# Order of the last pair of an MLP's first product, and one of two left sums moved to VectorE

## The chip, the cores and the metric

The kernel runs on one core of a Trainium2 chip. Five engines work side by side, each through its own queue in order: TensorE (PE in the profile; PEld is its loading of weights), VectorE (DVE), ScalarE (ACT), GpSimd (POOL) and SyncE (SP), whose queue here only issues DMAs. ACT issues DMAs too, for what it has just computed. The metric is the time of the whole program on the device in microseconds (us), lower being better.

## The reference

A transformer block on 2048 tokens of width 1024, in float32: attention with a memory carried over four segments, and then an MLP with 3584 inner features. The change lies in the MLP:

```python
def _B_ref(x, w1, b1, w2, b2):
    y = _layernorm(x, axis=-1)
    h = _gelu(jnp.einsum("bsd,df->bsf", y, w1) + b1)
    return jnp.einsum("bsf,fd->bsd", h, w2) + b2

h2 = h + _B_ref(_layernorm(h, axis=-1), B_w1, B_b1, B_w2, B_b2)
```

`h @ w2` is the MLP's second product, `y @ w1` its first.

## The kernel before

Every matrix product runs in three passes, since each operand x is split into a high part (`hi`, a cast to the format of the matmul, on ACT) and a low part (`x - hi`, a subtraction on DVE): high by high, high by low, low by high. Both products of the MLP use a scheme with seven block products in place of eight (Strassen's, in Winograd's form), so sums and differences of blocks are formed first.

*First product.* The tokens come in two halves. In each half, `Mixer.pair(j)` makes a pair of 128-row blocks of h, for j from 0 to 13, out of block products of 12 matmuls each. It is a generator that yields after every three matmuls, and the main loop hangs other work at these points, written (j, n): pair j, n-th yield. In the last pair of the second half (j = 13, `HP - 1`) there are 16 points: 0 to 3 multiply into the bank `bps`, then DVE reads `bps` (L1037); 4 to 7 multiply into the bank `dps`, then DVE reads it (L906), ACT applies the GELU (L899) and issues the store of h; 8 to 11 go on in `bps`, which DVE then reads; 12 to 15 go on in `dps`, which DVE then reads. A matmul that goes on in a bank waits for the read before it.

*Second product.* Class `Second` holds it. There are 112 products (`jobs`) of 21 matmuls, 56 for each of two halves of the inner features. In a half they go by groups of block products: "1" with "7", "6" with "5", "3" with "2", and "4". In a group the products of eight pairs of token blocks alternate. I number the products 0 to 111; the group of "6" and "5" is products 16 to 31 and 72 to 87. Its helpers are:

- `load_rows` and `rows_ahead` load rows of W2 into four buffers, on SP's queue. `presum` forms a sum of two rows on POOL where the block wants one (L1135). `fill` makes a piece of W2 of a row: the cast on ACT (L1143), the subtraction on DVE (L1144), and for some a store for later use on SP's queue (L1146). `fill_up(n, most)` makes all pieces due by product n, at most `most` of them.
- `load_items` loads the left blocks of h, named `hr`, into six buffers on SP's queue (L1171). `sums` forms their sums (L1189 for "1", L1192 and then L1193 for "6", L1198 for "3"), all on POOL. For "6" the result of L1192 is the left operand of "5" and the result of L1193 that of "6"; the latter is also stored (to `s2_dram`, shown as `s_dram`, at L1256) for the group of "3", and its buffer is loaded again once that store has landed.
- `prep(n)` makes the left operand of product n: a cast on ACT (L1212) and a subtraction on DVE (L1213).
- `add` adds a finished bank to one or two blocks of the output, on DVE (L1282). These blocks, `c`, are loaded by `ahead`.

`run` names, for each product n, first its matmuls and then `work(n)`: rows and loads on SP, sums due by product n + 2, `prep(n + 2)`, the additions of product n, the pieces of W2 due by now, and sums due by n + 4. Everything from the last part of the layer norm on is under `in_order()`, which binds each engine to the order in which the code names its instructions. So a line that is named earlier stands earlier in its engine's queue, and on SP's queue a DMA that waits for a buffer holds all that are named behind it.

Product 2, ("7", 0), goes on in the bank of product 0, so its first matmul waits for the additions of product 0. Of the 14 pieces of W2 that products 0 to 3 need, four remain for the last pair; two of them have rows in buffers of another pool (`APART`, shown as w2s).

Of the kernel before, what the change touches and what calls it, by code (L numbers as in the profile page):

```python
# [13 lines left out]
ALU = mybir.AluOpType  # L14
# [29 lines left out]
def build(tc, x, wq, wk, wv, wo, beta, w1, b1, w2, b2, out):  # L44
    nc = tc.nc
# [147 lines left out]
    def chain(*gens):  # L193
        for g in gens:
            yield from g
# [136 lines left out]
    def attention_pool(half):  # L332
        ab = acts["ab"] = tc.alloc_tile_pool(name=f"ab{half}", bufs=1, reuse_waits="tile")
        mask = acts["mask"] = ab.tile([P, 512], F32, name="mask")
        nc.gpsimd.memset(mask, 0.0)
        nc.gpsimd.affine_select(mask[:, 384:512], mask[:, 384:512], pattern=[[-1, P]],
                                compare_op=ALU.is_ge, fill=-1e9 / SCALE, base=0, channel_multiplier=1)
        acts["mz"] = ab.tile([P, NG * 132 + 96], F32, name="MZ")
        if half == 0:
            nc.gpsimd.memset(acts["mz"], 0.0)  # L340
        else:
            nc.sync.dma_start(acts["mz"], mz_dram)
# [350 lines left out]
    def load_x(half, sl, hts):  # L693
        for t in range(4):
            r0 = half * HT + (4 * sl + t) * P
            nc.sync.dma_start(hts[t], x[0, r0:r0 + P, :])
# [176 lines left out]
    HP = FB // 2  # L873
# [175 lines left out]
    class Second:  # L1049
# [129 lines left out]
        def sums(self, n, due):  # L1179
            tt = nc.gpsimd.tensor_tensor  # L1180
            while self.ns < self.ni and self.items[self.ns][0] <= due:
                at, s, g, p = self.items[self.ns]
                if at > n + 2 and self.came[s, g, p] >= n:
                    break
                r = {w: self.raws.pop((s, g, p, w)) for w in self.LOADS[g]}
                t = {w: x[0] for w, x in r.items()}
                self.ns += 1
                if g == "1":
                    tt(t["21"], t["11"], t["21"], op=ALU.subtract)  # L1189
                    src = ("1", "11"), ("7", "21")  # L1190
                elif g == "6":
                    tt(t["21"], t["21"], t["22"], op=ALU.add)  # L1192
                    tt(t["11"], t["21"], t["11"], op=ALU.subtract)  # L1193
                    self.later.append((s2_dram[p], t["11"]))
                    src = ("6", "11"), ("5", "21")
                    self.free.append(r["22"][1])
                elif g == "3":
                    tt(t["s2"], t["12"], t["s2"], op=ALU.subtract)  # L1198
                    src = ("3", "s2"), ("2", "12")
                else:  # L1200
                    src = ("4", "22"),
                for name, w in src:
                    self.srcs[s, name, p] = r[w]
# [95 lines left out]
    for half in range(2):  # L1299
        acts["zt"] = zt = tc.alloc_tile_pool(name=f"zt{half}", bufs=1, side="right")  # L1300
        attention_pool(half)
        first = None if half else opening()
        rest = attention(half, first)
        hts = [lnp.tile([P, D], F32, tag="ln", name="ht0", bufs=4) for _ in range(4)]
        ab = acts["ab"]
        load_x(half, 0, hts)

        def pre():
            for _ in range(PD):
                yield  # L1310
            for g in range(NG - 1):
                load_o(half, 1, g, ab)
                for _ in range(PS):
                    yield

        interleave(wo_first(half, hts, pre()), rest, RA, RH, RS)
        if half == 0:
            nc.sync.dma_start(mz_dram, acts["mz"])
        ab.release()
        zx = acts["zx"] = tc.alloc_tile_pool(name=f"zx{half}", bufs=1, side="right", reuse_waits="tile")  # L1320
        mq = tc.alloc_tile_pool(name=f"mq{half}", bufs=1, side="right", reuse_waits="tile")
        pp = tc.alloc_tile_pool(name=f"post{half}", bufs=1, reuse_waits="tile")
        hts1 = [pp.tile([P, D], F32, name=f"ht1{i}") for i in range(4)]
        acts["b2"] = pp.tile([P, D], F32, name="b2c")
        mixer = Mixer(half, mq)
        last_token = []

        def ready(t):
            steps = ln2_token(half, hts1, pp, t)
            if t < 3:  # L1330
                for _ in steps:
                    pass
            else:
                last_token.append(steps)

        second = wo_second(half, hts1, ready)
        load_x(half, 1, hts1)
        nc.sync.dma_start(acts["b2"], bass.AP(tensor=b2.tensor, offset=b2.offset, ap=[[0, P], [1, D]]))
        with in_order(mybir.EngineType.PE):
            interleave(hooked(second, lambda k: mixer.begin(), 57, 1),  # L1340
                       ln2(half, 0, hts, pp), 0.5)
        acts.pop("last")

        def ln2_last():
            yield
            next(last_token[0])
            side = ln2_combined(half, hts1)
            for n, _ in enumerate(side):
                if n == 1:
                    next(last_token[0])  # L1350
                yield

        order = ExitStack()
        order.enter_context(in_order())
        side, acc = ln2_last(), 0.0
        todo = {11: lambda: mixer.combine(0), 12: lambda: (mixer.fetch(1), mixer.made(0, "S2", "S1", "S3")),
                13: lambda: (mixer.made(0, "A22", "S4"), mixer.combine(1))}
        for _ in mixer.lead():
            acc += 0.4
            while side and acc >= 1.0:  # L1360
                acc -= 1.0
                if next(side, 0) == 0:
                    side = None
                    pp.release()
                    mp = mixer.mp = tc.alloc_tile_pool(name=f"m1{half}", bufs=1, side="right", reuse_waits="tile")
                    mixer.fetch(0)
            if mixer.step in todo and not side:
                todo.pop(mixer.step)()
        assert not todo

        if half == 0:
            for j in range(HP - 9):
                for _ in mixer.pair(j):
                    pass
            acts["ahead"] = ln1(1, 1)
            interleave(chain(*(mixer.pair(j) for j in range(HP - 9, HP))),
                       chain(ln1(1, 0, 2), islice(acts["ahead"], 3)), 0.17)
            mp.release()
            mq.release()
            zx.release()  # L1380
            zt.release()
        else:
            second = Second(mq)
            fill_at = [(j, 5) for j in range(HP - 8, HP - 2)] + [(HP - 3, 13), (HP - 2, 12), (HP - 2, 15), (HP - 2, 18),
                       (HP - 1, 1), (HP - 1, 9), (HP - 1, 13)]
            for j in range(HP):
                if j == HP - 1:
                    mp.release()
                    acts["sp"] = sp = tc.alloc_tile_pool(name="sp", bufs=1, side="right", reuse_waits="tile")
                for n, _ in enumerate(mixer.pair(j)):  # L1390
                    if (j, n) == (HP - 9, 8):
                        second.rows_ahead(-10)
                    if (j, n) == (HP - 1, 0):
                        second.load_items(-2)
                    if (j, n) in ((HP - 1, 6), (HP - 1, 10)):
                        second.sums(0, n // 10)
                    if (j, n) in ((HP - 1, 8), (HP - 1, 12)):
                        second.prep(n // 12)
                    if (j, n) in fill_at:
                        second.fill_up(-8, 1)  # L1400
                        second.rows_ahead(-10)
                    if (j, n) == (HP - 1, 1):
                        second.presum(second.nl)
                    if (j, n) == (HP - 1, 12):
                        second.ahead(-1)
            second.fill_up(-8, 1)
            second.rows_ahead(-10)
            second.prep(2)
            wp.release()
            acts["cl"] = cl = tc.alloc_tile_pool(name="cl", bufs=1, reuse_waits="tile")  # L1410
            cl.tile([P, 512], F32, tag="r", name="c", bufs=4)
            cl.tile([P, 512], F32, tag="w", name="c", bufs=12)
            acts["cx"] = cx = tc.alloc_tile_pool(name="cx", bufs=1, reuse_waits="tile")
            second.run()
        order.close()
# [24 lines left out]
```

## Time and profile before

| | |
|---|---|
| median of 3 runs | 2308.16 us (2304.3 to 2308.86) |
| the profiled execution | 2308.02 us |
| its span, first to last instruction | 2305.8 us |
| granted clock of TensorE | 1.000 |
| PE busy | 2273.6 us, 99% |
| DVE busy | 1546.7 us, 67% |
| ACT busy | 1224.5 us, 53% |
| POOL busy | 1067.9 us, 46% |

The first product of the second half of the tokens ends at about 1762 us, the second product runs from there to the end. In the profile, times are counted from the first instruction. A busy time says how long an engine worked, not whether anyone waited for it; what a stage is limited by is read from the waits of PE in it, which the next section shows.

### The profile page before, as it was taken

The page shows a single profiled execution, that of the slowest core. Times are in us where ns is not written, and L with a number is a line of the kernel's source. Part 1 is how long each engine was busy: PE and PEld are TensorE (multiplying, and loading weights), DVE is VectorE, ACT ScalarE, POOL GpSimd, SP SyncE. Part 2 cuts the span into 40 slices and gives each one's busy share as a digit, 9 for nine tenths or more (in the row PEclk, how much of TensorE's full clock was granted, in tenths as well). Part 3 has the DMA queues.
Part 4 walks back from the last instruction along what each step waited for, and adds up shares of the span by engine and source line. Part 5 has one row for each costly group of instructions (what it writes and reads, how often), then busy time and mean ns, then how long its engine had stood idle before and what let it go on. Part 6 is the DMA issues. An engine that isn't in the chain of part 4 may idle for free.

```text
span 2305.8 us, 35327 instructions
## 1 busy us (share of the span) xinstructions
PE 2273.6 (99%) x11769; PEld 1890.2 (82%) x11769; DVE 1546.7 (67%) x3271; ACT 1224.5 (53%) x2549; POOL 1067.9 (46%) x1084
## 2 busy tenths in 40 slices
PE   8999999999999999999999999999999999999999
PEld 6888888878888888888888877888887878888887
DVE  6777777776655565777777777665566756566553
ACT  5777777775453445777777775363333223322221
POOL 5444555554244442555555546253444554155340
PEclk9999999999999999999999999999999999999999
DMA  6333333335466654433333344466658976476762
GB/s 177 102 84 92 92 85 84 90 110 184 139 208 174 183 169 141 113 92 86 85 89 87 85 113 147 154 210 174 178 174 276 327 243 217 155 244 219 257 235 91
DMA packets 322719, 355.36 MB, mean 154 GB/s; under 512 B 26190, under 2 KB 218730, under 8 KB 322538
## 3 DMA queue, kind: packets, MB, share of 16 engines
q1 hardware_dynamic: 259370, 316.40, 45.2%
q10 hardware_dynamic: 63168, 36.71, 5.3%
q8 instruction: 93, 1.52, 0.3%
q14 instruction: 88, 0.72, 0.1%
HBM read 226.59 MB, written 76.09 MB: 131 GB/s over the span
## 4 chain that ended last, share of the span: by engine, by line
PE 84%; ACT 4%; DMA 3%; DVE 3%; POOL 3%; issue 2%; SPq 1%; ACTq 0%; DVEq 0%; POOLq 0%
PE po L1272 20%; PE bps L882 9%; PE cps L882 7%; PE dps L882 6%; PE ppt L573 5%; PE po L593 5%; PE pqk L541 3%; PE vps L115 2%; PE vps L116 2%; PE vps L117 2%; PE kps L115 2%; PE kps L116 2%; PE kps L117 2%; PE qps L116 2%; PE qps L115 2%
## 5 line engine op out<-in xcount | busy, mean ns | idle before, releaser
L557 POOL TENSOR_SCALAR pr<-pr,nm,gate 128x128 f32<-128x128 f32 (+3 forms) x512 | 321.0, 636 | 355.1 <-DVE nm L554 272.4
L550 ACT ACTIVATE pr<-pr,mx 128x256 f32<-128x256 f32 (+3 forms) x512 | 287.5, 562 | 166.2 <-DVE mx L542 163.2
L580 DVE TENSOR_TENSOR ptl<-ppt,pth 128x512 fp32r<-128x512 f32 (+1 forms) x384 | 227.2, 599 | 73.9 <-ACT pth L575 68.7
L542 DVE CUSTOM_DVE_ANT_0 pr<-pqk,mask 128x256 f32<-128x256 f32 (+3 forms) x512 | 242.8, 484 | 42.7 <-PE pqk L541 40.1
L573 PE MATMUL ppt<-ident,pr 128*128 128x128 f32 x1280 | 223.6, 277 | 2.3 <-POOL pr L557 1.5
L575 ACT CAST pth<-ppt 128x512 fp32r<-128x512 f32 (+1 forms) x384 | 194.2, 517 | 35.5 <-PE ppt L573 29.4
L1282 DVE TENSOR_TENSOR c<-c,po 128x512 f32<-128x512 f32 x160 | 105.3, 682 | 143.8 <-PE po L1272 141.1
L573 PEld LDWEIGHTS ppt<-ident,pr 128*128 128x128 f32 x1280 | 164.1, 140 | 33.5 <-DVE ptl L580 2.8
L541 PE MATMUL pqk<-ks,qs 96*128 96x256 f32 (+3 forms) x512 | 161.4, 316 | 0.0
L593 PE MATMUL po<-ptl,vs 128*64 128x512 f32 (+3 forms) x512 | 154.2, 311 | 3.0 <-DVE ptl L580 2.9
L92 POOL TENSOR_TENSOR wl<-wr,wh 128x1024 fp32r<-128x1024 f32 x52 | 124.4, 2393 | 69.8 <-PE pqk L541 25.9
L593 PE MATMUL po<-pth,vs 128*64 128x512 f32 (+3 forms) x512 | 155.5, 326 | 0.3 <-ACT pth L575 0.2
L1272 PE MATMUL po<-w2h,zh 128*128 128x512 f32 x378 | 121.0, 390 | 2.3 <-DVE zh L1213 1.3
L1135 POOL TENSOR_TENSOR w2r<-w2r 128x512 f32<-128x512 f32 x54 | 85.0, 1586 | 66.3 <-DMA w2r<-in_B_w 43.7
L541 PEld LDWEIGHTS pqk<-ks,qs 96*128 96x128 f32 x512 | 96.2, 188 | 21.5
L882 PE MATMUL bps<-zh,sb 128*128 128x512 f32 x336 | 111.1, 391 | 1.2 <-DVE u L1037 1.2
L882 PE MATMUL bps<-zh,sa 128*128 128x512 f32 x336 | 110.8, 390 | 0.0
L115 PE MATMUL kps<-yh,wh 128*128 128x512 f32 (+1 forms) x264 | 110.3, 418 | 0.0
L994 POOL TENSOR_TENSOR s<-r 128x512 f32<-128x512 f32 x28 | 43.8, 1564 | 143.2 <-DVE sa L1010 87.5
L115 PE MATMUL vps<-yh,wh 128*128 128x512 f32 x256 | 109.4, 427 | 0.2 <-ACT omt L521 0.2
L115 PE MATMUL qps<-yh,wh 128*128 128x512 f32 x256 | 106.8, 417 | 0.0
L1272 PE MATMUL po<-w2h,hl 128*128 128x512 f32 x322 | 103.0, 390 | 0.0
(238 smaller groups left out, 6642.9 us busy)
## 6 DMA issues: line engine op xcount, KB each, us to landing
hr<-h_dram SPq DMA_DIRECT2D x112, 448.0 KB, 5.4
w2r<-in_B_w SPq DMA_DIRECT2D x122, 256.0 KB, 4.4
r<-in_B_w SPq DMA_DIRECT2D x56, 512.0 KB, 4.6
h_dram<-ht ACTq DMA_DIRECT2D x84, 256.0 KB, 3.7
ks<-kh SPq DMA_DIRECT2D x256, 64.0 KB, 2.0
qs<-qh SPq DMA_DIRECT2D x256, 64.0 KB, 2.0
wr<-in_A_wo SPq DMA_DIRECT2D x32, 512.0 KB, 4.0
wx<-in_B_w SPq DMA_DIRECT2D x56, 256.0 KB, 3.4
```

The source lines that it names most:

```text
L115: nc.tensor.matmul(ps, ah, bh, start=first, stop=False)
L116: nc.tensor.matmul(ps, ah, bl, start=False, stop=False)
L541: nc.tensor.matmul(pqk[:, :n], u["qs"][j][:, i * P:(i + 1) * P], u["ks"][j][:, 0:n], start=True, stop=True)
L542: nc.vector.tensor_tensor_reduce(out=st["pr"][:, offs[i]:offs[i] + n], in0=pqk[:, :n], in1=mask[:, 512 - n:512], op0=ALU.add, op1=ALU.min, ...
L550: nc.scalar.activation(pi, pi, AF.Exp, bias=mx[:, i:i + 1], scale=-1.0, accum_out=mx[:, 4 + i:5 + i])
L557: nc.gpsimd.tensor_scalar(pi, pi, nm[:, 4 + k:5 + k], gate[:, 1, 4 * g + j:4 * g + j + 1], op0=ALU.mult, op1=ALU.mult)
L573: nc.tensor.transpose(ppt[:, o:o + P], pr[:, offs[i] + jk * P:offs[i] + (jk + 1) * P], ident)
L575: acts["pth"] = n, nc.scalar.copy(pth[:, base:base + w], ppt[:, :w])
L580: nc.vector.tensor_tensor(o, x0, x1, op=ALU.subtract)
L593: nc.tensor.matmul(po[:, P * jk:], v, st[part][:, koff[jk]:koff[jk] + w], start=(jk, part) == (0, "pth"), stop=(jk, part) == (2, "ptl"))
L882: nc.tensor.matmul(ps, x_[:, c, :], y_[:, c, :], start=first and c == 0 and n == 0, stop=last and c == 3 and n == 2, skip_group_check=True)
L1272: nc.tensor.matmul(ps, x_[:, k], y_[k], start=opens and k == 0 and i == 0, stop=closes and k == self.KP - 1 and i == 2, skip_group_check=True)
```

## The change

There are four edits.

1. In the last pair, pieces of W2 are named later: the one at point 1 moves to point 4, the one at point 9 to point 13, and the one at point 13 to behind the pair, where two are now made instead of one.
2. `prep(1)` moves from point 12 to point 11, ahead of the second read of `bps` in the queues of ACT and DVE.
3. At point 1, `rows_ahead` is called by itself before `presum`, as no piece is made there any more.
4. In the sums of "6" (16 times in all) the first of the two runs on DVE instead of POOL. The second stays on POOL.

```diff
                 elif g == "6":
-                    tt(t["21"], t["21"], t["22"], op=ALU.add)
+                    nc.vector.tensor_tensor(t["21"], t["21"], t["22"], op=ALU.add)
                     tt(t["11"], t["21"], t["11"], op=ALU.subtract)
...
             fill_at = [(j, 5) for j in range(HP - 8, HP - 2)] + [(HP - 3, 13), (HP - 2, 12), (HP - 2, 15), (HP - 2, 18),
-                       (HP - 1, 1), (HP - 1, 9), (HP - 1, 13)]
+                       (HP - 1, 4), (HP - 1, 13)]
...
-                    if (j, n) in ((HP - 1, 8), (HP - 1, 12)):
-                        second.prep(n // 12)
+                    if (j, n) in ((HP - 1, 8), (HP - 1, 11)):
+                        second.prep(n // 11)
                     if (j, n) in fill_at:
                         second.fill_up(-8, 1)
                         second.rows_ahead(-10)
                     if (j, n) == (HP - 1, 1):
+                        second.rows_ahead(-10)
                         second.presum(second.nl)
                     if (j, n) == (HP - 1, 12):
                         second.ahead(-1)
-            second.fill_up(-8, 1)
+            second.fill_up(-8)
             second.rows_ahead(-10)
             second.prep(2)
```

## The prediction

> **What bounds the kernel now.** I read the page's busy times first, then the list of waits of PE from 1700 us to the end, then the timeline of each engine around each wait. The columns of a timeline row are start, duration, engine, line, operation, tiles, and in brackets the idle time before it and what ended it.
>
> ```profile
> PE 2273.6 (99%) x11769; PEld 1890.2 (82%) x11769; DVE 1546.7 (67%) x3271; ACT 1224.5 (53%) x2549; POOL 1067.9 (46%) x1084
> ```
> ```profile
> PE po L1272 <- DVE c L1282: 1.7, 1, 1.7
> PE po L1272 <- DVE zh L1213: 1.3, 2, 0.9
> PE bps L882 <- DVE u L1037: 1.2, 1, 1.2
> PE po L1272 <- ACT zh L1212: 1.0, 1, 1.0
> PE po L1272 <- DVE hl L1213: 0.8, 1, 0.8
> ```
> ```profile
> 1756.78 0.47 PE L882 MATMUL bps<-zh,sb 128*128 128x512 f32 x1 [1.18 <-DVE u L1037]
> 1768.62 0.72 PE L1272 MATMUL po<-w2h,zh 128*128 128x512 f32 x2 [0.93 <-DVE zh L1213]
> 1774.90 0.47 PE L1272 MATMUL po<-zh,zl 128*128 128x512 f32 x1 [1.66 <-DVE c L1282]
> 1855.45 0.39 PE L1272 MATMUL po<-w2l,hl 128*128 128x512 f32 x1
> 1855.68 0.39 PE L1272 MATMUL po<-w2h,hl 128*128 128x512 f32 x1
> 1857.05 0.50 PE L1272 MATMUL po<-w2h,zh 128*128 128x512 f32 x1 [0.98 <-ACT zh L1212]
> 1858.17 0.73 PE L1272 MATMUL po<-w2h,zh 128*128 128x512 f32 x2 [0.39 <-DVE zh L1213]
> ```
>
> PE is busy 99%, and all that it waits for after 1700 us is 1.7 + 1.3 + 1.2 + 1.0 + 0.8 = 6.0 us. That is the ceiling of any gain here. Three waits stand at the junction of the two products of the MLP (1.18, 0.93, 1.66: 3.77 us together), two more (1.37 us) in the group of "6", at its third pair's first product. Without a wait a matmul starts 0.23 us after the one before (1855.45, 1855.68). The profiled execution took 2308.02 us, 0.14 under the median of the three runs shown (2308.16); those runs spread over 4.6 us, so about 0.2% (4.6 us) is what a measurement of this kernel tells from no change. The sums below are against 2308.02.
>
> **The junction, part by part.** A piece of W2 is a cast on ACT, a subtraction on DVE and a store on SP's queue; a left operand ("prep") is a cast and a subtraction. I call the pieces by their place among the last four: A, B, C, D. Before, DVE's order is A, read of bps (L1037), read of dps (L906), left operand 0, B, read of bps (L906), left operand 1, C, read of dps, D, left operand 2, additions of product 0. After it is: read of bps, A, read of dps, operand 0, operand 1, read of bps, B, read of dps, C, D, operand 2, additions. Nothing is added or removed, on SP the store of B goes behind four loads of c, and the extra look for rows ahead finds none left to load (all fourteen were named by the pair before), so it costs nothing.
>
> ```profile
> 1755.34 0.69 DVE L1144 TENSOR_TENSOR zl<-w2r,zh 128x512 fp32r<-128x512 f32 x1 [1.85 <-ACT zh L1143]
> 1755.95 0.68 DVE L1037 TENSOR_TENSOR u<-bps,p1r 128x512 f32<-128x512 f32 x1
> ...
> 1760.78 2.60 DVE L1144 TENSOR_TENSOR zl<-w2s,zh 128x512 fp32r<-128x512 f32 x1
> ...
> 1766.16 2.41 DVE L1213 TENSOR_TENSOR zh<-hr,zh 128x896 fp32r<-128x896 f32 x1 [2.17 <-ACT zh L1212]
> ...
> 1769.09 0.68 DVE L906 TENSOR_TENSOR ht<-dps,u 128x512 f32<-128x512 f32 x1
> ```
> ```profile
> 1760.36 2.47 POOL L1189 TENSOR_TENSOR hr<-hr 128x896 f32<-128x896 f32 x1 [0.45 <-DMA hr<-h_dram]
> 1765.49 2.13 POOL L1189 TENSOR_TENSOR hr<-hr 128x896 f32<-128x896 f32 x1 [2.66 <-DMA hr<-h_dram]
> ```
> ```profile
> 1770.97 0.62 ACT L1143 CAST zh<-w2r 128x512 fp32r<-128x512 f32 x1 [0.44 <-ACT ht L899]
> 1771.49 0.94 ACT L1212 CAST zl<-hr 128x896 fp32r<-128x896 f32 x1
> ```
>
> First wait: the read at L1037 stands behind A (1755.34 to 1756.03). Ahead of it, it needs only PE's products, and PE goes on without a gap: 1.2 us earlier. Second wait: operand 1 comes a product sooner, so the first wait of product 1 goes too, 0.9 us. The third wait, however, is for the additions of product 0 on DVE (L1282), and these stand at the end of one chain through DVE and ACT. Its length decides, whatever PE does ahead of it.
>
> That chain is ruled by POOL. DVE operations with both inputs in SBUF that meet a running sum of POOL end after it: B was ready at 1760.78, POOL's second sum ran until 1762.83, and B ended at 1763.38; operand 1 ended at 1768.57, 0.95 after POOL's third sum (1767.62). DVE operations that read a bank are not held. In the new order operand 1 takes B's place at 1760.8. POOL's second sum asks at 1760.36, when its load lands, so I let POOL go first again: operand 1 ends at 1762.83 + 0.95 = 1763.8, the read of bps at 1764.45 (0.68). From the end of such a read to the end of the cast behind its GELU and store is 1.8 us (1769.77 to 1771.59), so B's subtraction is ready at 1766.25, in the middle of POOL's third sum, and ends 0.55 behind it: 1768.15. Read of dps: 1768.8. Cast of C: 1770.55 (+1.8); cast of D 0.5 later; cast of operand 2 0.9 later, 1772.0; its subtraction (1.08, the smallest L1213 below) 1773.1; two additions (1.28, as in the pair quoted below) 1774.4; PE some 0.1 later at 1774.5, against 1774.90. **Term 1: -0.4 us.** The 2.1 us that the first two waits give up are paid back at the third, where PE then waits some 4 us at once. Cover gone at DVE costs nothing elsewhere: the products that follow wait for nothing until 1857.05.
>
> [...]
>
> **The left sum of the "6" on DVE.** Sixteen times (eight pairs, two halves) the first of two sums moves from POOL to DVE.
>
> ```profile
> L1192 POOL TENSOR_TENSOR hr<-hr x16: 2112/2134/3055, 1817.4 to 2165.6; 128x896 f32<-128x896 f32 x16
> L1213 DVE TENSOR_TENSOR hl<-hr,hl x38: 1077/1091/2845, 1759.7 to 2288.8; 128x896 fp32r<-128x896 f32 x38
> ```
>
> On DVE the nearest row of that size costs 1.08 us against 2.13: 1.05 us less in the chain sum, sum, cast, subtraction, product. No row shows a DVE sum there; it is bounded by 1.08 free and 2.85 (the longest L1213, held by POOL). I take 1.08, since POOL has nothing else at these places but to wait for it. What it adds is a wait: DVE runs in order, so the sum now stands behind the additions of a product that has just ended and behind the pieces of W2 of that product, where POOL, ahead of PE, took it as soon as its loads landed. Behind it on DVE wait the next left operand (which needs it anyway), the next additions, two pieces of W2, and through them SP's queue, whose load of a row waits for the piece that frees its buffer, with the store of the left sum and the next loads behind it.
>
> First half. The places that matter are the second and the third pair, where the sums come behind three and two pieces of W2:
>
> ```profile
> 1837.07 1.28 DVE L1282 TENSOR_TENSOR c<-c,po 128x512 f32<-128x512 f32 x2 [2.47 <-PE po L1272]
> 1838.27 4.60 DVE L1144 TENSOR_TENSOR w2l<-w2r,w2h 128x512 fp32r<-128x512 f32 x3
> ```
> ```profile
> 1853.58 2.45 POOL L1193 TENSOR_TENSOR hr<-hr 128x896 f32<-128x896 f32 x1
> ```
> ```profile
> 1846.36 0.76 SPq L1256 DMA_DIRECT2D s_dram<-hr  x1
> ...
> 1854.09 1.27 SPq L1171 DMA_DIRECT2D hr<-h_dram  x3
> ```
>
> The three pieces took 4.60 us, held by POOL's sums; with POOL waiting for DVE they take 3 x 0.6 + 0.1. From 1837.95 (0.4 earlier): pieces to 1839.8, DVE sum to 1840.9, POOL's sum (2.12) to 1843.1, cast (0.95) to 1844.1, subtraction to 1845.3, additions to 1846.6, two pieces to 1848.0, operand (1.08, after its cast) to 1849.35, one addition and two pieces to 1851.3, the next DVE sum to 1852.4, POOL's to 1854.6 against 1856.03, its cast to 1855.6. The product could start at 1855.5 (1855.68 + 0.23 - 0.4); its third matmul, due at 1856.0, waits for the subtraction, 1856.7. With the cast's 0.1 that is 0.8 lost. Before, the first matmul started 1.14 late (1857.05 for 1855.91) and the third 0.68 behind that (1858.17 for 1857.49): 1.8. **Term 2: -1.0 us.** The store goes at 1847.75 instead of 1846.36, and the three loads behind it (7.7 us later, when it has landed) as much later; the next left operand then misses its product by about 0.35: **term 3: +0.35.** From then on each round is 1.05 us shorter.
>
> Second half, same place:
>
> ```profile
> 2106.74 1.28 DVE L1282 TENSOR_TENSOR c<-c,po 128x512 f32<-128x512 f32 x2 [0.71 <-PE po L1272]
> ```
> ```profile
> 2114.24 0.58 SPq L1256 DMA_DIRECT2D s_dram<-hr  x1
> ...
> 2121.88 1.27 SPq L1171 DMA_DIRECT2D hr<-h_dram  x3
> ```
> ```profile
> 2121.74 2.12 POOL L1193 TENSOR_TENSOR hr<-hr 128x896 f32<-128x896 f32 x1
> ```
> ```profile
> 2126.03 0.70 PE L1272 MATMUL po<-w2h,hl 128*128 128x512 f32 x2
> ```
> ```profile
> 2153.48 1.09 DVE L1213 TENSOR_TENSOR hl<-hr,hl 128x896 fp32r<-128x896 f32 x1 [5.40 <-ACT hl L1212]
> ```
> ```profile
> 2154.71 0.65 PE L1272 MATMUL po<-w2h,hl 128*128 128x512 f32 x2
> ```
>
> Here POOL had done both sums by 2108.0, ahead of PE. On DVE the sum comes only at 2111.0, and the same steps end POOL's sum of the next pair at 2125.2 instead of 2123.86; the subtraction is ready at 2127.3, where the third matmul wanted and got it at 2126.03. With the cast 0.6 late and the subtraction 0.6 more that is 1.2, and the old trace lost 0.1: **term 4: +1.1 us.** The store slips from 2114.24 to 2117.75, the loads from 2121.88 to some 2124.8, with a lighter DMA queue (7.0 us to land instead of 7.6, my estimate between the rows of such stores, 6.2 to 9.0). I count no more for it: the PE is 1.1 later and each round 1.05 shorter; the smallest slack of a later round is 0.14 (a subtraction that ended at 2154.57 for a matmul at 2154.71).
>
> Sum: -0.4 - 1.0 + 0.35 + 1.1 = +0.05 us. **Forecast 2308.1 us**, no measurable change.
>
> **The rivals.** [...]
>
> *Slower: SP's queue behind the late pieces.* The place is the store of the left sum behind the load of a row. If it slips X and nothing damps it, each half loses X - 1.05 - 0.14 by the fourth round; with X = 3.5 in both halves (2117.75 less 2114.24) that is 2 x 2.3, without terms 2 to 4: 2308.0 - 0.4 + 4.6 = 2312.2. It is slower by 0.2% from X = 3.7 on. For it speak the in-order queue and the small slack; against it the 1.05 us per round.
>
> *The sum on DVE gains nothing,* held by POOL's sums of W2 at every place (towards 2.85 us): terms 2 and 4 become 0 and +1.6, 2309.2.
>
> **How the numbers follow.** Forecast 0.5, the early port 0.2 (a third of it under 2303.5), SP's queue 0.2 (three quarters of it over 2312.7, since POOL can hold the pieces as well), no gain on DVE 0.1. With the forecast's own spread of 2 us: faster by over 0.2% 0.14, within 0.65, slower 0.21. The range, 2303.2 to 2312.6, reaches from the best of the early port to the slower rival; the forecast's own is 2306 to 2310.
>
> **What would show it.** PE's waits at 1756 and 1768 gone and one of about 4 us before product 2, still ended by the additions at L1282. The left operand 1 about 2 us long beside POOL's second sum. L1192 on DVE at 1.1 us, its start ended by the engine's own order and not by a load. The first store of the "6" in the second half 3 us later in PE's time. The forecast is wrong if the wait before product 2 is under 1 us (early port), or if PE waits in every round of the "6" (SP's queue).

## The result, and the profile after

The changed kernel took 2311.88 us (median of 13 runs, 2308.57 to 2314.6) against 2308.16 for the kernel before (13 runs): a ratio of 1.0018 with a 95% interval of 1.0011 to 1.0025, 3.7 us slower by the medians. A second set of runs, told of below, gave 1.0010 (1.0001 to 1.0019). The forecast was no change, 2308.1 us; the time lies in the upper part of the range, and its cause was not among the terms. The profiled execution took 2311.88 us, its span was 2310.1 us.

The busy times and PE's waits from 1700 us on, in the changed kernel (us in total, times, longest):

```profile
PE 2276.2 (99%) x11769; PEld 1891.5 (82%) x11769; DVE 1552.5 (67%) x3287; ACT 1225.6 (53%) x2549; POOL 1031.8 (45%) x1068
```
```profile
PE po L1272 <- DVE c L1282: 4.8, 3, 3.6
PE po L1272 <- DVE hl L1213: 0.6, 2, 0.4
PE po L1272 <- DVE zh L1213: 0.4, 1, 0.4
PE po L1272 <- ACT zh L1212: 0.3, 1, 0.3
PE po L1272 <- ACT hl L1212: 0.2, 1, 0.2
```

PE's waits add up to 6.3 us where they were 6.0, and PE's busy time grew by 2.6 us with the same 11769 matmuls. So the list of waits alone does not show what was lost. Both kernels run the same matmuls in the same order, so I compare the start of each matmul in the two traces. The changed kernel's lateness grows as follows:

| place | lateness at its end, us | added there, us |
|---|---|---|
| up to the last pair of the first product (1752.49 in the trace before) | 2.13 | 2.13 |
| from there to the start of product 2 | 1.36 | -0.77 |
| product 2 itself | 2.83 | +1.47 |
| products 3 to 17 | 2.83 | 0 |
| products 18 and 19 | 2.97 | +0.14 |
| products 20 to 73 | 2.35 | -0.62 |
| products 74 and 75 | 4.32 | +1.97 |
| the rest | 4.26 | -0.06 |

The first row is read from one matmul, here in the kernel before and then in the changed one:

```profile
1752.49 0.39 PE L882 MATMUL bps<-zh,sb 128*128 128x512 f32 x1
```
```profile
1754.62 0.39 PE L882 MATMUL bps<-zh,sb 128*128 128x512 f32 x1
```

Ahead of it the programs name the same work in the same order; the traces of the kernels below have this matmul between 1.12 us early and 1.97 us late, whether they hold parts of the change or not. So that row is no cost of the change that I could show, and what has to be explained is the other +2.13.

**The junction.** Timeline of the changed kernel around product 2, first PE, then ACT, POOL and DVE, and a table by stretches (busy time with the number of instructions for PE, PEld, DVE, ACT, POOL; then the granted clock, the DMA share, GB/s):

```profile
1776.26 0.77 PE L1272 MATMUL po<-zh,zl 128*128 128x512 f32 x1 [3.57 <-DVE c L1282]
1776.82 0.63 PE L1272 MATMUL po<-zl,zl 128*128 128x512 f32 x1
1777.25 1.05 PE L1272 MATMUL po<-zh,zl 128*128 128x512 f32 x2
```
```profile
1763.32 0.95 ACT L1212 CAST zh<-hr 128x896 fp32r<-128x896 f32 x1 [2.06 <-DMA hr<-h_dram]
```
```profile
1764.58 4.88 POOL L1189 TENSOR_TENSOR hr<-hr 128x896 f32<-128x896 f32 x2 [0.21 <-DMA hr<-h_dram]
```
```profile
1764.31 1.09 DVE L1213 TENSOR_TENSOR zh<-hr,zh 128x896 fp32r<-128x896 f32 x1 [1.91 <-ACT zh L1212]
...
1767.91 2.10 DVE L1144 TENSOR_TENSOR zl<-w2s,zh 128x512 fp32r<-128x512 f32 x1 [1.91 <-ACT zh L1143]
...
1774.84 1.28 DVE L1282 TENSOR_TENSOR c<-c,po 128x512 f32<-128x512 f32 x2
```
```profile
1772.00:1776.30 4.30, 0.73 (x5) 0.30 (x3) 3.77 (x6) 3.47 (x5) 0.00 (x0) 0.96 0.97 313
1776.30:1779.40 3.10, 3.10 (x8) 2.44 (x9) 3.01 (x4) 0.00 (x0) 0.00 (x0) 0.51 0.94 365
1779.40:1783.00 3.60, 3.60 (x17) 2.97 (x16) 0.22 (x1) 0.00 (x0) 2.90 (x2) 1.00 0.93 324
```

The two small waits are gone, and one of 3.57 us stands before product 2, as forecast. But behind it PE does 8 matmuls in 3.10 us at a granted clock of 0.51, where the next 3.60 us hold 17 at 1.00: the starts are 0.43 us apart (1776.82, 1777.25) instead of 0.23. This is the +1.47 inside product 2, and PE counts it as busy.

**The "6".** Timeline of the changed kernel at products 15 to 19, DVE, POOL and PE:

```profile
1842.91 1.08 DVE L1192 TENSOR_TENSOR hr<-hr 128x896 f32<-128x896 f32 x1
...
1849.51 2.38 DVE L1144 TENSOR_TENSOR w2l<-w2r,w2h 128x512 fp32r<-128x512 f32 x2
1851.82 2.17 DVE L1213 TENSOR_TENSOR hl<-hr,hl 128x896 fp32r<-128x896 f32 x1
1853.92 0.67 DVE L1282 TENSOR_TENSOR c<-c,po 128x512 f32<-128x512 f32 x1
```
```profile
1844.07 2.12 POOL L1193 TENSOR_TENSOR hr<-hr 128x896 f32<-128x896 f32 x1 [3.81 <-DVE hr L1192]
1846.15 6.90 POOL L1135 TENSOR_TENSOR w2r<-w2r 128x512 f32<-128x512 f32 x4
```
```profile
1854.74 0.47 PE L1272 MATMUL po<-w2h,hl 128*128 128x512 f32 x1 [0.60 <-DVE c L1282]
...
1860.02 0.50 PE L1272 MATMUL po<-w2h,zh 128*128 128x512 f32 x1 [0.26 <-ACT zh L1212]
```

The row at 1854.74 is new: product 18, the first ("5", 0), goes on in the bank of product 16 and waits for its addition, the last DVE row. POOL stood 3.81 us for DVE's sum, and four of its sums of W2 (L1135), which stand behind its second sum in the queue, then ran in one lump of 6.90 us. Beside it two pieces took 2.38 us on DVE and a left operand 2.17, and the addition of product 16 stands behind them. The same picture stands in the second half, at product 74.

### The profile page after: what moved, and what is told of

Read it like the earlier page. It is cut to its first block, busy times and chain, and to the rows that moved or that the text cites. A ratio compares the mean times of both kernels' runs of the same rounds, so it can differ in the third digit from the quotient of the medians.

```text
span 2310.1 us, 35315 instructions
## 1 busy us (share of the span) xinstructions
PE 2276.2 (99%) x11769; PEld 1891.5 (82%) x11769; DVE 1552.5 (67%) x3287; ACT 1225.6 (53%) x2549; POOL 1031.8 (45%) x1068
## 4 chain that ended last, share of the span: by engine, by line
PE 86%; DVE 4%; ACT 4%; POOL 2%; DMA 2%; issue 2%; SPq 0%; ACTq 0%; POOLq 0%; DVEq 0%
PE po L1272 20%; PE bps L882 9%; PE cps L882 7%; PE dps L882 6%; PE ppt L573 5%; PE po L593 5%; PE pqk L541 3%; PE vps L115 2%; PE vps L116 2%; PE vps L117 2%; PE kps L115 2%; PE pwo L117 2%; PE pwo L116 2%; PE kps L116 2%; PE pwo L115 2%; PE kps L117 2%
## 5 line engine op out<-in xcount | busy, mean ns | idle before, releaser
L1135 POOL TENSOR_TENSOR w2r<-w2r 128x512 f32<-128x512 f32 x54 | 86.9, 1625 | 55.6 <-DMA w2r<-in_B_w 55.0
```

## The experiments

The table has, for each kernel, the ratio to the kernel before with its 95% interval, and what the start of PE's matmuls shows in its trace against the first trace of before: from the last pair (1752.49) to the start of product 3, and from there to the end. The last column is the wait before product 2, and how many slow matmuls follow it (those whose next one starts over 0.35 us later, where 0.23 is usual). Each trace is one execution.

| kernel | ratio | junction, us | product 3 to end, us | wait before product 2 |
|---|---|---|---|---|
| before | 1 | 0 | 0 | 1.66, none slow |
| the change, first run | 1.0018 (1.0011 to 1.0025) | +0.70 | +1.43 | 3.57, 7 slow |
| after_again | 1.0010 (1.0001 to 1.0019) | -0.26 | +2.00 | 2.45, 8 slow |
| e1_order_only | 1.0003 (0.9994 to 1.0011) | +0.60 | -0.39 | 2.95, 8 slow |
| e2_sum_only | 1.0006 (0.9998 to 1.0015) | -0.33 | +1.33 | 1.63, none slow |
| e3_warm | 1.0007 (0.9998 to 1.0016) | -1.01 | +1.89 | 0.27, none slow |
| e4_sum_late_pairs | 0.9997 (0.9988 to 1.0006) | -2.49 | -1.51 | 1.65, none slow |
| e7_both_mended | 1.0001 (0.9992 to 1.0010) | -1.32 | -2.05 | 0.27, none slow |
| e9_both_sums_early | 1.0002 (0.9993 to 1.0011) | -1.76 | -1.28 | 1.6, none slow |
| e5_addition_first | 0.9987 (0.9978 to 0.9996) | -3.82 | +0.67 | none |
| e6_first_and_late_sum | 0.9985 (0.9976 to 0.9994) | -4.59 | -0.88 | none |
| e10_first_and_both | 0.9976 (0.9965 to 0.9986) | -4.59 | -2.23 | none |

In kernels with added lines the line numbers are higher by some (L1273, L1283). A ratio of 0.0001 is 0.23 us, and the intervals are some 2 us to either side, so between neighbours of the table the ratios decide nothing; there I go by what the traces show, and the ratios only have to agree.

**e1_order_only: edits 1 to 3 without the sum on DVE.**

```diff
-                    nc.vector.tensor_tensor(t["21"], t["21"], t["22"], op=ALU.add)
+                    tt(t["21"], t["21"], t["22"], op=ALU.add)
```

> The new order of the last pair alone (pieces of W2 and left operand 1 at their new places); the left sum of group "6" stays on POOL. Theory (the order gains its two waits, 1.48 + 1.19 us, loses 1.76 us at the wait before product 2, and then 1.43 us because PE comes out of a wait of over 3.5 us with a granted clock of about one half for 3 us): the junction costs +0.5 us, nothing more is lost in the rounds, so about 2308.7 us against 2308.2 before, and matmuls of product 2 again 0.43 us apart for seven of them. Rival (the DVE sum is harmless and the whole loss is the order's): about 2312 us. Second rival (PE's later start up to 1756 us, +2.3 us in the changed kernel's trace, belongs to the order by way of the program's layout): matmuls ahead of 1756 us start about 2.3 us later here too and the time is about 2311.

Measured: 2307.82 us (before 2307.61). PE's wait before product 2, and the stretches from there on:

```profile
1774.35 0.47 PE L1272 MATMUL po<-zh,zl 128*128 128x512 f32 x1 [2.95 <-DVE c L1282]
```
```profile
1774.40:1775.60 1.20, 1.20 (x6) 0.98 (x7) 1.20 (x2) 0.00 (x0) 0.00 (x0) 1.00 1.08 361
1775.60:1778.70 3.10, 3.10 (x9) 2.44 (x8) 1.80 (x3) 0.00 (x0) 0.00 (x0) 0.54 0.97 361
```

The theory's picture: the slow matmuls are there with the order alone, the junction costs +0.60, and there is no new wait in the rounds. The rival that puts the whole loss on the order falls, and so does the one by the program's layout: PE is 0.5 us late before the last pair, not 2.3.

**e2_sum_only: edit 4 alone, in the kernel before** (the line above the other way round).

> Only the left sum of group "6" on DVE instead of POOL; the last pair as before. Theory (product 18 and product 74 go on in the bank of the product before the last, whose addition stands on DVE behind the late sum): new waits of 0.8 us and 0.7 us at these two, the next products gain or lose -0.6 and +1.2 us, so about +1.5 us, 2309.7, with no slow matmuls at the junction. Rival (the sum is free): 2308.2 and no new wait of PE. Second rival (the start of all work up to 1756 us moves by +2.3 us with any change of the program): about 2312.

Measured: 2309.78 us. The new wait is there, and again before product 74:

```profile
1852.96 0.47 PE L1272 MATMUL po<-w2h,hl 128*128 128x512 f32 x1 [0.59 <-DVE c L1282]
```

From product 3 to the end the trace has +1.33 us. By their ratios the two halves of the change cost 0.7 + 1.4 = 2.1 us together, neither of them certain by its interval alone.

**e3_warm: the changed kernel with something for PE to do in the wait.** It computes the same output and 12 matmuls more.

```diff
+        def warm(self, count):
+            bh, _ = self.slot(0)
+            ps = bank("warm", "av", 1)
+            for _ in range(count):
+                nc.tensor.matmul(ps, bh[0][:, 0:P], bh[1], start=True, stop=True, skip_group_check=True)
...
             for n in range(len(self.jobs)):
+                if n == 2:
+                    self.warm(12)
```

> The changed kernel with 12 further matmuls, whose result nothing reads, in PE's queue between product 1 and product 2, where PE waits 3.6 to 4.8 us for the additions of product 0. Theory (the seven matmuls 0.43 us apart are PE's clock after a long idle time): they vanish, product 2 still starts at the same point behind the additions, and the time is 1.4 us under the changed kernel, about 2310.4. Rival (these matmuls are slow because of what the other engines and DMAs do there): the spacing stays at 0.43 us and the time is that of the changed kernel, 2311.9, or above it.

Measured: 2308.99 us, ratio 1.0007 where the changed kernel has 1.0018 and 1.0010. PE at the junction:

```profile
1771.31 2.88 PE L1290 MATMUL warm<-w2h 128*128 128x512 f32 x12
1774.46 0.47 PE L1272 MATMUL po<-zh,zl 128*128 128x512 f32 x1 [0.27 <-DVE c L1282]
1774.77 0.39 PE L1272 MATMUL po<-zl,zl 128*128 128x512 f32 x1
1775.00 0.63 PE L1272 MATMUL po<-zh,zl 128*128 128x512 f32 x2
```

Product 2 still starts when the additions are done, but its matmuls follow each other 0.23 us apart (1774.77, 1775.00), at a granted clock of 1.00. The DMAs, the pieces and the other engines' work are the same there, so it is PE's idle time that makes them slow.

The mean granted clock that is on record for every execution says the same of the runs without a trace. The traces in which the clock fell once have 0.999, those in which it did not have 1.000. The changed kernel shows 0.999 or 0.998 in 22 of 24 executions and e1_order_only in 10 of 11; the kernel before shows 1.000 in 72 of the 84 that ran beside the experiments, e3_warm in 10 of 11, and all the other kernels together in 63 of 74. So the fall goes with the merged wait, and goes away with e3_warm's matmuls. (That it can come elsewhere too, the last section shows.)

**e4_sum_late_pairs: the sum on DVE from the third pair on.**

```diff
-                    tt(t["21"], t["21"], t["22"], op=ALU.add)
+                    (nc.vector if p > 1 else nc.gpsimd).tensor_tensor(t["21"], t["21"], t["22"], op=ALU.add)
```

> The kernel before with the left sum of group "6" on DVE only from the third pair of blocks on (the first two stay on POOL). Theory (the loss sits in the two halves' first rounds of group "6", where the row loads are still late): no new wait at products 18 and 74, time as before, 2308.2 within 0.5. Rival (every round pays, by SP's queue or by DVE's own order): about +1.5 us, 2309.7, with waits spread over the rounds.

Measured: 2305.85 us, with no wait at products 18 and 74. On POOL the sums of W2 come one by one again, and the addition of product 16 is early; POOL and DVE:

```profile
1841.38 1.29 POOL L1135 TENSOR_TENSOR w2r<-w2r 128x512 f32<-128x512 f32 x1 [2.40 <-DMA w2r<-in_B_w]
1844.32 2.13 POOL L1135 TENSOR_TENSOR w2r<-w2r 128x512 f32<-128x512 f32 x1 [1.64 <-DMA w2r<-in_B_w]
```
```profile
1845.21 0.68 DVE L1282 TENSOR_TENSOR c<-c,po 128x512 f32<-128x512 f32 x1
```

So the loss of edit 4 sits in the first two of eight pairs in each half. The ratio (0.9997) is that of before within its interval. The trace is 1.5 us ahead from product 3 to the end, but that is not shown to be a gain of the sum: 0.8 us of it stand at product 19, where e1_order_only, with this sum on POOL, gains 0.6 too, and 1.0 at product 57, where executions differ (see below); 0.4 are lost between.

**after_again: the changed kernel once more,** beside the kernel before.

> The changed kernel once more, unaltered, beside the kernel before. The trace of its first run shows +2.0 us from the junction on and +2.3 us that PE already had at 1458 us, where the two programs are the same. Theory (that early part differs from execution to execution and is no cost of the change; the order alone and the sum alone, which measured 0.7 and 1.4 us above the median of before by their ratios, add up): about 2.0 us above before, ratio 1.0009, with an early part anywhere between -1 and +2.5 us. Rival (the early part belongs to the changed program): again 4.1 us above before, ratio 1.0018, and again over 2 us at 1458 us.

Measured: 2309.36 us, ratio 1.0010, as the theory had it: nearer to the sum of the two halves than the first run. PE was 1.9 us late at 1458 us, near what the rival asked for. But e5_addition_first, e7_both_mended and e9_both_sums_early, where that part is the same, are 1.4 to 1.8 us late there without being slower than before, so it doesn't go with the changed program. A part of it in e9_both_sums_early is a fall of the clock at 1390 us, across which PE's lateness grows by 1.3 us; why else executions differ there by some 3 us stays open.

**e7_both_mended: the changed kernel with e3's 12 matmuls and e4's condition.**

> The changed kernel with 12 further matmuls between products 1 and 2, which nothing reads, and with the left sum of "6" on DVE from the third pair of blocks on only. Theory (the cold clock, 1.4 us, and the bank waits at products 18, 19, 74 and 75, 2.1 us with their followers, are all that the change loses): no matmul 0.43 us apart, no wait at products 18 and 74, 3 us under the changed kernel and between 0 and 1.5 us under the kernel before. Rival (something else costs too): still 1 us or more above the kernel before.

Measured: 2307.06 us, ratio 1.0001 (before 2307.01). The waits of PE from 1700 us on:

```profile
PE po L1272 <- DVE hl L1213: 0.9, 1, 0.9
PE po L1272 <- DVE c L1282: 0.3, 1, 0.3
```

No slow matmul, no wait at 18 or 74: with the two causes taken away the loss is gone. A gain of up to 1.5 us, which the theory allowed, did not show in the time, though the trace is ahead (-1.32 and -2.05).

**e9_both_sums_early: is it POOL's standing still, or DVE's order?** The order of before, the first sum on DVE everywhere, the second too in the first two pairs.

```diff
-                    tt(t["21"], t["21"], t["22"], op=ALU.add)
-                    tt(t["11"], t["21"], t["11"], op=ALU.subtract)
+                    nc.vector.tensor_tensor(t["21"], t["21"], t["22"], op=ALU.add)
+                    (nc.gpsimd if p > 1 else nc.vector).tensor_tensor(t["11"], t["21"], t["11"], op=ALU.subtract)
```

> The order of the kernel before; the first left sum of "6" on DVE in all pairs (as in e2_sum_only), and in the first two pairs of each half the second one as well, so that POOL no longer stands still for DVE there. Theory (the loss comes about on POOL: its second sum waits 3.8 us for DVE's first, four of its sums of W2 pile up behind and then run for 6.9 us in a lump, which makes two pieces and a left operand on DVE late by 1.1 us each and with them the addition that product 18 needs): no lump, the pieces and the operand at 1.2 and 1.1 us, no wait at products 18 and 74; 1.5 to 2 us under e2_sum_only, so about the time of before or up to 0.7 us under it. Rival (DVE's own order makes the addition late): the waits of 0.75 us at products 18 and 74 stay, 1.4 us above before.

Measured: 2307.64 us, ratio 1.0002. POOL and DVE at the place shown of the changed kernel:

```profile
1843.40 1.29 POOL L1135 TENSOR_TENSOR w2r<-w2r 128x512 f32<-128x512 f32 x1 [12.20 <-DMA w2r<-in_B_w]
1845.49 1.30 POOL L1135 TENSOR_TENSOR w2r<-w2r 128x512 f32<-128x512 f32 x1 [0.80 <-DMA w2r<-in_B_w]
```
```profile
1846.75 2.38 DVE L1144 TENSOR_TENSOR w2l<-w2r,w2h 128x512 fp32r<-128x512 f32 x2
1849.05 1.08 DVE L1213 TENSOR_TENSOR hl<-hr,hl 128x896 fp32r<-128x896 f32 x1
1850.06 0.68 DVE L1282 TENSOR_TENSOR c<-c,po 128x512 f32<-128x512 f32 x1
```

DVE has more to do here, and yet the addition of product 16 is in time and the waits are gone: the late addition did not come from DVE's own load. One part of the expectation missed: the two pieces still take 2.38 us. From the additions ahead of the first sum to the end of this addition DVE takes 13.46 us, against 14.68 in e2_sum_only; 1.09 of the 1.22 us gained are the operand (1.08 for 2.17), beside which the lump no longer runs, and only 0.13 are the shorter way of the second sum. The operand alone outweighs the 0.75 us by which product 18 was late, so the lump on POOL was the cause.

**e5_addition_first: another order of the last pair.** The additions of product 0 stand ahead of B, C and D on DVE.

```diff
-                       (HP - 1, 1), (HP - 1, 9), (HP - 1, 13)]
+                       (HP - 1, 4)]
...
+                    if (j, n) == (HP - 1, 13):
+                        second.prep(2)
+            got = second.product(0)
+            second.add(*got)
-            second.fill_up(-8, 1)
+            second.fill_up(-8)
             second.rows_ahead(-10)
-            second.prep(2)
```

(`run` then starts at `work(0)` without its additions; `prep(1)` and the extra `rows_ahead` are as in the change.)

> Another order of the last pair (the left sum of "6" on POOL): piece A at point 4 and the left operand of product 2 at point 13, then product 0 and its two additions are named, and only behind these the pieces B, C, D. Theory (the wait before product 2 is for the additions of product 0, which stood behind B, C, D on DVE): that wait and the slow matmuls after it vanish, and what is left is at most a wait inside product 2 for D: 2 to 4 us under the kernel before. Rival (the pieces come as late as the additions did, since POOL's sums hold them anyway): the wait moves into product 2 with the same 3 us, and the time is that of before or up to 1 us above it.

Measured: 2303.82 us against 2307.01, ratio 0.9987: 3.0 us, between 0.9 and 5.1. There is no wait before product 2 at all. The additions on DVE, and then PE's waits from 1700 us on:

```profile
1770.87 1.27 DVE L1283 TENSOR_TENSOR c<-c,po 128x512 f32<-128x512 f32 x2
1772.80 1.29 DVE L1144 TENSOR_TENSOR zl<-w2s,zh 128x512 fp32r<-128x512 f32 x2 [0.66 <-ACT zh L1143]
```
```profile
PE po L1273 <- DVE hl L1213: 1.8, 3, 1.0
PE po L1273 <- DVE c L1283: 0.5, 1, 0.5
PE po L1273 <- DVE zh L1213: 0.4, 1, 0.4
PE po L1273 <- DVE w2l L1144: 0.2, 1, 0.2
```

Of the gain at the junction 0.6 us are lost again by product 17. The wait before product 18 (0.5 us) stands here and in e6_first_and_late_sum (0.6 us) too, although both sums of the first two pairs are on POOL: in the trace of e5_addition_first three pieces of W2 take 6.25 us on DVE beside POOL's sums. So edit 4 is one way to a late addition at this place, not the only one.

**e6_first_and_late_sum** adds e4's condition to it.

> The order of e5_addition_first, and the left sum of "6" on DVE from the third pair of blocks on. Theory (the DVE sum gains some 0.7 us at product 19 where no addition stands behind it late, and loses nothing): 0.7 us under e5_addition_first. Rival (nothing to gain from the engine of this sum): the time of e5_addition_first.

Measured: 2303.50 us, ratio 0.9985. The 0.3 to 0.5 us under e5_addition_first are less than the intervals, so this settles nothing.

**e10_first_and_both** has both left sums of "6" on DVE in all pairs, in that order.

> The order of e5_addition_first, and both left sums of "6" on DVE in all pairs. Theory (a sum is 1.1 us on DVE and 2.1 on POOL, and POOL waits for nothing then): the waits at products 18 and 19 that e5_addition_first shows (1.6 us with the product's third matmul) go or shrink to under 0.5 us, 1 to 1.5 us under e5_addition_first's ratio of 0.9987, so about 0.9982. Rival (DVE, with 2.2 us more in each round of "6", becomes late there): waits in the rounds and a time above e5_addition_first's.

Measured: 2301.72 us against 2307.10, ratio 0.9976 (0.9965 to 0.9986): some 5.5 us faster than before, and the lowest ratio of all these kernels, though its interval overlaps those of e5_addition_first and e6_first_and_late_sum. The list of PE's waits from 1700 us on has one row left:

```profile
PE po L1273 <- DVE hl L1213: 0.6, 1, 0.6
```

The waits at products 18 and 19 are gone, as the theory had it; the rival, DVE becoming late, did not come about.

## Why the prediction was wrong

**The step "where PE then waits some 4 us at once".** The wait is there (3.57 us, forecast as some 4), and it was counted only as the waits that it replaced, less what the chain gains. What failed is the sentence behind it, that cover gone "costs nothing elsewhere". Behind the merged wait the granted clock falls to about half (0.51 over 3.10 us in the change, 0.54 over 3.10 in e1_order_only), which costs 1.5 us in the change and 1.6 in e1_order_only. This is the largest single term of the loss, and it was put at nothing in the sum.

**Term 1, -0.4 us, up to the start of product 2.** The first trace has -0.77, but that is one execution. The chain from the matmul at 1752.49 to product 2, against the first trace of before, is -0.77, -1.89, -1.03, -1.04, -1.35 in five traces with the new order (mean -1.2) and 0, -0.37, -2.50, -1.80 in four with the old one (mean -1.2). The order's gain at this point is lost in what executions differ by. The two waits which the change was seen to take away are not there in every execution of the old order either: e4's trace has neither. The step which let POOL's second sum go first did not hold in the first trace: operand 1 was not held (1.09 us at 1764.31), since its cast waited 2.06 us for the load, and the subtraction began 0.27 us ahead of POOL's second sum. B was held as foreseen (2.10, beside POOL's sum; the next piece, with no sum beside it, took 0.69), and the read of bps at 1765.31, beside a sum too, was not (0.69). In after_again, e1_order_only and e3_warm POOL does go first, operand 1 takes 3.0 us, and B is not held (0.69). So which of the two is held differs from execution to execution, with the landing of a load.

**Terms 2 and 3, -1.0 and +0.35.** Measured +0.14 at products 18 and 19 together, and 0 at 21. At product 19 alone PE gains 0.7, which has the size of most of term 2; but e1_order_only gains 0.6 there with the sum on POOL, so little of it is shown to be the sum's. Before it stands the wait for the bank at 18, +0.85 with the matmuls behind it, which was not seen. The step that failed is "I take 1.08, since POOL has nothing else at these places but to wait for it": 1.08 was right for the sum itself (the median of the sixteen is 1.08, the longest 1.09), but POOL has more to do than to wait for it: four sums of W2 stand behind its wait. The working gave the two pieces 1.4 us and the operand 1.1; they took 2.4 and 2.2. And among those who wait behind DVE's sum it named "the next additions" without asking which product goes on in their bank.

**Term 4, +1.1.** Measured +1.97 at products 74 and 75: +1.09 at 75, the term as forecast, and ahead of it the same bank wait, +0.88 at 74. The store of the left sum slips by 3.2 us in PE's time here (5.55 in the trace, 2.35 of it PE's own lateness), against 3.5 forecast:

```profile
2119.79 0.42 SPq L1256 DMA_DIRECT2D s_dram<-hr  x1
```

**The other 0.6 us gained between products 20 and 73** stand at product 57, where PE waits 0 to 1.1 us for a left operand in the traces of all the kernels; I don't put them to the change.

**The rivals.** SP's queue, the slower rival, had a time near the one measured (2312.2 for 2311.88), but by luck and not by its mechanism: PE does not wait in each round, and between products 20 and 73 its lateness changes at product 57 alone. That the sum on DVE gains nothing has terms near the measured ones (0 and +1.6, where +0.14 and +1.97 were measured), but is wrong for the sum (1.08 us) and half right in its reason: POOL held other instructions of DVE (the two pieces, 2.38 us, and the operand, 2.17), not this one. The chance of 0.2 called the early port, and the lower end of the range with it, stood for operand 1 going ahead of POOL's second sum. That order came in the first trace, and operand 1 took 1.09 us, but the gain did not come: the loads landed later than in the trace before (POOL's second sum, which waits for one, began at 1764.58 and not at 1760.36). No run shows a port; what the runs show is how long operand 1 took, 1.09 us where it began ahead of POOL's sum and 3.0 where POOL began first.

**The ceiling of 6.0 us** counts PE's idle time only. By the starts of the matmuls a wait costs some 0.2 us more: before product 2 one of 1.66 us puts 2.04 between two starts in place of 0.23. In e10_first_and_both's trace the gain from 1752.49 to the end is 6.8 us.

Against +0.05 forecast the change's own part is +2.1 us in the first trace and +1.7 in the second; the ratios say 4.2 (2.5 to 5.8) and 2.3 (0.2 to 4.4). That the first ratio is above its trace's part is left unexplained.

## What to carry to other kernels

Three waits of TensorE that become one need not cost the same time: ask how long the merged wait is (3.57 us here), and what the clock does behind it (0.51 over 3.10 us here), and if it can't be shortened, try giving TensorE something to do in it. When an instruction moves to another engine, the engine it leaves may have to stand still for it (3.81 us here), and what is queued behind that wait then comes in a lump (6.90 us); here the loss was gone when both sums of the first two pairs moved, or neither. To shorten a wait for a bank, look first at what stands ahead of the bank's reader on its own queue: naming the additions ahead of work that is due later gained more than all else tried here (3.0 us in e5_addition_first).

## What the runs showed of the hardware

The granted clock fell to about half at waits of TensorE of 2.45, 2.95 and 3.57 us (three traces of three), and not at those of 1.6 to 1.7 us before product 2 (before, e2, e4, e9). It did not always fall at once: in the trace with 2.95 us the first six matmuls still ran at 1.00 for 1.2 us, in the one with 3.57 us the slow ones began with the first. Each fall lasted 3.4 us by the clocks of the stretches (4.00 us at 0.57, in the rows below, are 3.44 us at 0.50, the clock in the last rows of this section, and the rest at 1.00); it slowed 7 or 8 matmuls and cost 1.5 to 1.6 us. The repeated run of the changed kernel, its wait and the stretch behind it:

```profile
1774.97 0.48 PE L1272 MATMUL po<-zh,zl 128*128 128x512 f32 x1 [2.45 <-DVE c L1282]
```
```profile
1775.00:1779.00 4.00, 4.00 (x11) 3.18 (x12) 3.02 (x4) 0.00 (x0) 0.00 (x0) 0.57 1.04 346
```

The length of one wait is not all that counts. In the attention, far ahead of the change, every trace has a stretch in which PE waits 1.1 us and works little around it. In ten traces the clock stayed at 1.00 there; in e9_both_sums_early (and in e6_first_and_late_sum) it fell to half behind it, again for 3.4 us:

```profile
1388.66 0.30 PE L395 MATMUL pm<-mzh,pqh 128*128 128x132 f32 x1 [1.10 <-DVE rg L483]
```
```profile
1387.00:1390.70 3.70, 2.42 (x15) 1.66 (x14) 3.29 (x13) 3.29 (x8) 3.70 (x3) 1.00 0.02 4
1390.70:1394.10 3.40, 3.40 (x15) 2.71 (x13) 2.48 (x7) 0.99 (x5) 2.00 (x3) 0.50 0.60 190
```

So no length of wait separates the two here: before product 2 the shortest wait with a fall was 2.45 us and the longest without one 1.66, but a stretch whose longest wait was 1.1 us had a fall in two of twelve traces. A length that is safe, and what decides between two executions of the same stretch, no run shows.
